# FNet mixing and a SoLU block on one core: three moves in the order of the steps

## The chip, the cores and the metric

The kernel runs on one core of a Trainium2 chip. The metric is the device time of one execution in microseconds. All times below are microseconds unless they say ns. The engines are named as in the profile: PE (TensorE, matmuls) with PEld (its weight loads), DVE (VectorE), ACT (ScalarE), POOL (GpSimd), and SP (SyncE, which here only issues DMAs).

## The reference

The first part is a Fourier mixing of `x`, 8 batches of 3136 rows by 256 features; its real part, as 25088 rows, goes through a block with 1024 hidden features.

```
X = fft(fft(x, axis=1), axis=2).real            # (8, 3136, 256) -> 25088 rows
h = X @ w_in                                    # 256 -> 1024
solu = h * softmax(h)
ln = (solu - mean) / sqrt(var + 1e-6) * g_ln
out = ln @ w_out                                # 1024 -> 256
```

All is in fp32.

## The kernel before, in words

**Pairs and units.** Two batches are a pair; there are four, numbered 0 to 3 in the code (`pairs`, and in the text here). The transform over the 3136 rows is split as 49 x 64. The *first transform* (length 49) is a matmul of the folded input with the table `F`; the *second* (length 64, with twiddles, table `T`) gives for one frequency `k1` the 128 x 256 tile `q`. Symmetry leaves 25 values of `k1`, so a pair has 25 *units* and the kernel 100. A unit stands for two results (`signs` 0 and 1), save for `k1 = 0`, which has one.

**Steps.** The program is one list of steps, written out by hand (`tc.manual_schedule()`): each engine runs its instructions in the order in which the code names them. Step `i` treats unit `i` in its middle part and other units in other parts. Steps 0 to 4 (`whole` is 4) form a first loop in which finished tiles are transposed on PE; from step 5 on the second loop runs:

- PE: `up` (two matmul groups, `h = q W_in`, line 272, into two PSUM banks); the second transform of unit `i + 2` (line 244); the product with `w_out` of unit `i - 5` (`Down`, line 446), as seven smaller products p1 to p7 by Strassen's scheme, in the order p1, p4, p5, (first transform), p6, p2, p3, p7.
- DVE: `even` (`ev`, line 278), two `join`s (line 286), two operations that finish an output (lines 503 and 505), the fold of a part of a chunk (below), two products (line 301), and a transpose in blocks (line 372).
- ACT: exponentials (294), squares (308), copies out of PSUM.
- POOL: the mirror of a part of a chunk, the four sums `S` of unit `i - 4` that p5, p6, p3 and p7 of the next step read (line 439), `rs`, and DMAs with indices.
- SP: in every even step `move_blocks` issues 16 DMAs (uT<-v, 128 KB each, line 408), in every odd one the output stores; also the DMAs named below. All of SP's DMAs go in the order in which they are issued.

`up` of the next step needs both PSUM banks free: the first after `ev`, the second after the second join.

**The next pair's first transform.** It runs inside the steps of the pair before. The rows of a pair are cut into 8 chunks (`NC`); chunk `c` has a start step `SUMS[p][c]`, two steps after the chunk before it. With `a` the step minus this start:

- `a` 0 and 1: POOL adds the mirrored rows, half a chunk in each (`add_mirror`, line 142). Each waits for the last product of the unit before (`behind`).
- `a` 1 and 2: DVE folds the features of that half (`fold_part`: lines 149, 150 and 174), and ACT copies one column.
- `a` 2: the load of chunk `c + 2` is issued, `xa` on SP (line 125) and `xb` on POOL (line 127). Chunks 0 and 1 are loaded at the first step of the pair before.
- `a` 3 and 4: PE transforms the halves (`transform1`, line 216), into one PSUM bank that the second transform uses too; ACT copies the result to `z`, and after the second half SP stores the chunk to a buffer in DRAM (`keep`, zd<-z, line 224).

`ahead` is called with "mirror", "fold" and "load". In steps 0 to 3 all three are called at the end of the step; in step 4 the mirror is called ahead of the block transpose (`turn_both`), and fold and load at the end.

**Turn.** `turn` reads the buffer in DRAM back with other axes on the partitions (g<-zd, line 232, issued on POOL), five values of `k1` at a time. The first is issued at the end of the step that lies 4 ahead of the pair's first (steps 21, 46 and 71); the second transform reads it two steps later (23, 48 and 73).

With start steps 3, 27 and 53, the halves of chunk 7 are transformed in steps 20 and 21 for pair 1, in 44 and 45 for pair 2, and in 70 and 71 for pair 3.

Of the kernel before, what the change touches and what calls it, by code (L numbers as in the profile page):

```python
# [26 lines left out]
NC = NH // CH  # L27
# [16 lines left out]
def kernel(  # L44
# [139 lines left out]
    def transform1(pr, s):  # L184

        c, l = divmod(2 * s, CH)
        if s == 0:
            pr.zd = dram.tile([ZR, NH, D], FP32, tag="zd", name="zd")  # L190
        if l == 0:

            if pr.p or c < 2:
                pr.z = zpool.tile([ZR, CH, D], FP32, tag="z", name="z")
            elif c < 4:
                if c == 2:
                    pr.z_u = fpool.tile([P, 2, FF], FP32, tag="u", name="z_u", bufs=1)
                pr.z = pr.z_u[0:ZR, c - 2].rearrange("p (l d) -> p l d", l=CH)
            elif c < 6:
                pr.z = Ws.rearrange("p (h w) c k -> h p (w c k)", h=2)[c - 4, 0:ZR].rearrange("p (l d) -> p l d", l=CH)  # L200
            elif c == 6:
                pr.z = S_tiles[1][0:ZR, 0:2].rearrange("p a c k -> p (a c k)").rearrange("p (l d) -> p l d", l=CH)
            else:
                pr.z = gpool.tile([P, KG, D], FP32, tag="g", name="z_g")[0:ZR, 0:CH, :]
            pr.zs[c] = pr.z
        y = pr.y[c]
        ps = result(0 if pr.p else s).rearrange("p (l d) -> p l d", l=2)
        if s == NH // 2 - 1:
            parts = [(ps[0:ZR, 0], y[:, l], 0), (ps[0:ZR, 1], pr.y0[:, 0], 1), (ps[0:ZR, 1], y[:, l + 1], 2)]
        else:  # L210
            parts = [(ps[0:ZR], y[:, l : l + 2], 0)]
        pr.done.append(s)
        first = True
        for o, i, t in parts:
            for h, cs in enumerate((EVEN, ODD)):
                nc.tensor.matmul(o[..., cs], F[:, 2 * t + h, :], i[..., cs], start=first, stop=True,  # L216
                                 skip_group_check=True)
                first = False
        nc.scalar.copy(pr.z[:, l : l + 2, :], ps[0:ZR])
        if l == CH - 2:  # L220
            keep(pr, c, slice(0, ZR if pr.p else 4 * KG))
# [295 lines left out]
    def first_out(t):  # L517
        if t.w == 0:
            t.batch.out = fpool.tile([P, 2, D], FP32, tag="ot0", name="ot0", bufs=2)
        return t.batch.out[:, t.w]  # L520

    def scale(t, s, ps):
        t.ot[s] = fpool.tile([P, D], FP32, tag="ot1", name="ot1", bufs=3) if s else first_out(t)
        nc.scalar.mul(out=t.ot[s], in_=ps, mul=t.rs[:, s : s + 1])
# [170 lines left out]

    SUMS = [None] + [[f + 2 * c for c in range(NC)] for f in (3, 27, 53)]

    def ahead(pr, i, work, after=None):  # L700

        for c in range(NC):
            a = i - SUMS[pr.p][c]
            if work == "load" and (i == (pr.p - 1) * NK and c < 2 or a == 2 and c + 2 < NC):
# [9 lines left out]
                          mybir.DependencyInfo(mybir.DependencyClass.Sync, mybir.DependencyReason.DATA),  # L714
                          reason="two operands at a time from SBUF")

    def ahead_pe(pr, i):

        for c in range(NC):
            half = i - SUMS[pr.p][c] - 3  # L720
            if half in (0, 1):
                transform1(pr, c * CH // 2 + half)

# [6 lines left out]
    with tc.manual_schedule():  # L730
# [80 lines left out]
        whole = WHOLE  # L811
# [21 lines left out]
        def other_pairs(i, do, *a):  # L833
            cur = units[i]
            if cur.p + 1 < NP:
                do(pairs[cur.p + 1], i, *a)
# [3 lines left out]
        for i in range(whole + 1):  # L840
            cur = units[i]
            prv = units[i - 1] if i else None
            if prv:
                turn_whole(prv)
            for s in cur.signs:
                join(cur, s)
            if prv and i < whole:
                for o, ps in prv.wait:
                    nc.vector.tensor_copy(out=o, in_=ps)
            for s in cur.signs:  # L850
                expo(cur, s)
            if prv and i == whole:
                for o, ps in prv.wait:
                    nc.scalar.copy(o, ps)
            if i == 0:

                weights.narrow_out(3)
            for s in cur.signs:
                product(cur, s)
                if i < whole and s == 0:  # L860
                    square(cur, s)
            if i == 1:
                weights.centre()
                weight_sums()
            if i < whole:

                begin(i + 1)
                if 1 in cur.signs:
                    square(cur, 1)
                stats(cur)  # L870
                power(cur)
            else:
                for s in cur.signs:
                    square(cur, s)
                other_pairs(i, ahead, "mirror", cur)
                turn_both(cur)
                stats(cur)
                power(cur)
            if i == 0:
                turn(first, 1, nc.sync)  # L880
            for work in ("mirror", "fold", "load") if i < whole else ("fold", "load"):
                other_pairs(i, ahead, work)

        def by_seven(i):
# [6 lines left out]
        for i in range(whole + 1, len(units) + lag + 1):  # L891
            cur = units[i] if i < len(units) else None
            prv = units[i - 1] if whole < i - 1 < len(units) else None
            old = units[i - lag] if i < len(units) + lag else None
            seven = by_seven(i - lag)
            kept = units[i - lag - 1] if i >= lag + 1 else None

            if kept:
                store(kept, 0)
            if cur:  # L900
                enter(i)
                even(cur, up(cur, 0))
                cur.odd = up(cur, 1)
                second_transform(i + 2)
            if seven:
                new = Down(old, fresh)
                fresh = False
                new.p1()
                new.seed()
            if i == len(units):  # L910
                for s in prv.signs:
                    square(prv, s)
            if prv:
                stats(prv)
            if seven:
                new.p4()
                new.p5()
                new.keep_p()
            elif old:
                plain = [(s, down(old, s, result(s + 1)[:, 0:D])) for s in old.signs]  # L920
            if cur:
                other_pairs(i, ahead_pe)
            if seven:
                new.p6()
                new.keep_x()
                new.p2()
                new.keep_c()
            elif old:
                for s, ps in plain:
                    scale(old, s, ps)  # L930
            if prv and prv.batch.shared and prv.w:
                prv.batch.mix()
            if cur:
                for s in cur.signs:
                    join(cur, s)
            if seven:
                new.p3()
                new.p7()
                new.finish()
            if cur:  # L940
                other_pairs(i, ahead, "mirror")
            if by_seven(i + 1 - lag):
                sums(units[i + 1 - lag], prv, nc.vector if i > len(units) else nc.gpsimd)
            if i % 2 == 0 and whole < i - 1 < len(units) - 2:
                batches[i // 2 - 1].place()
                move_blocks(batches[i // 2 - 1], slice(0, 2))
            if prv:
                power(prv)
            if kept and 1 in kept.signs:
                store(kept, 1)  # L950
            if cur:
                other_pairs(i, ahead, "fold")
                for s in cur.signs:
                    expo(cur, s)
                for s in cur.signs:
                    product(cur, s)
                if i < len(units) - 1:
                    for s in cur.signs:
                        square(cur, s)
                turn_both(cur)  # L960
                if cur.p == 0 and i in (5, 8, 11):
                    turn(first, (i + 1) // 3)
                for pr in pairs[1:]:
                    turn_parts(pr, i - pr.p * NK)
                other_pairs(i, ahead, "load")
            if i in (len(units), len(units) + 1):
                w = i - len(units)
                if w == 0:
                    batches[-1].place()
                move_blocks(batches[-1], slice(w, w + 1), (nc.sync, nc.gpsimd) if w else (nc.sync,))  # L970
# [82 lines left out]
```

## Time and profile before

| | |
|---|---|
| median of 3 runs | 1151.1 (1149.79 to 1153.33) |
| the profiled execution | 1150.92 |
| its span, first to last instruction | 1149.1 |
| mean granted clock of PE | 0.994 |
| a step with a first transform / without | 11.0 / 10.13 |
| busy share PE / DVE / ACT / POOL | 96% / 86% / 70% / 70% |

A row of the timeline gives the start in us, the duration in us, the engine, the line, the operation, output<-input, the shapes and a count; in brackets stands the engine's idle time ahead of it and what ended that. A row of the waits gives the engine, the line and tile, what it waited for, then the total in us, how often, and the longest. A row of the chain gives start, duration and what the end of the program hung on at that time. The step lengths are the distances between the first `up` matmuls of neighbouring steps.

### The profile page before, as it was taken

The numbers are of one execution on the slowest core, as the hardware profiler recorded it, in microseconds if no ns is written. First come the engines' busy times: TensorE is split into PE (matmuls) and PEld (weight loads), VectorE is DVE, ScalarE is ACT, GpSimd is POOL, SyncE is SP. The second block draws the span as 40 slices with busy tenths as digits, with TensorE's granted clock in tenths as the row PEclk, the third lists the DMA queues.
The fourth block names the chain that finished last, engine by engine and source line by source line (L and its number), as shares of the span: only waits on it lengthen the run. The fifth ranks groups of instructions, "written<-read, shape, count | busy, mean of one in ns | idle before, by whom it ended". The sixth has DMA issues, their size and how long they took to land.

```text
span 1149.1 us, 21936 instructions
## 1 busy us (share of the span) xinstructions
PE 1098.1 (96%) x7026; PEld 877.3 (76%) x7026; DVE 993.0 (86%) x1440; ACT 799.3 (70%) x1945; POOL 799.9 (70%) x698
## 2 busy tenths in 40 slices
PE   2988999999899999999999999999989999999998
PEld 1555787887688778778888787877868778888887
DVE  7889898898789988988888998898878999898983
ACT  4567777777566777777766777777766777777761
POOL 3036788875786888876778788876498576766673
PEclk9999999999999999999999999999999999999999
DMA  9772698776878779966869798876587676865664
GB/s 237 208 193 56 147 193 199 179 150 145 157 162 170 196 171 182 192 152 147 168 142 196 162 193 186 198 178 149 128 149 152 141 158 133 148 142 113 141 138 116
DMA packets 459889, 185.78 MB, mean 162 GB/s; under 512 B 427158, under 2 KB 441758, under 8 KB 459776
## 3 DMA queue, kind: packets, MB, share of 16 engines
q1 hardware_dynamic: 446016, 146.23, 62.1%
q0 software_dynamic: 13760, 38.16, 12.6%
q8 instruction: 57, 0.93, 0.3%
q14 instruction: 56, 0.46, 0.1%
HBM read 44.78 MB, written 38.80 MB: 73 GB/s over the span
## 4 chain that ended last, share of the span: by engine, by line
PE 85%; DMA 5%; DVE 4%; issue 2%; ACT 2%; POOL 1%; SPq 1%; POOLq 0%; DVEq 0%
PE ps_m L446 49%; PE ps_h L272 27%; PE ps_m L216 4%; PE ps_m L244 4%; DMA room<-in_x_dram 2%; DMA g<-zd 1%; DVE h L286 1%; DVE u L301 1%; DMA F<-in_f_tab_dram 1%; ACT h L308 1%; PE wps L660 1%; POOL S L439 0%; DVE ev L278 0%; DVE y L150 0%; DMA zd<-z 0%
## 5 line engine op out<-in xcount | busy, mean ns | idle before, releaser
L272 PE MATMUL ps_h<-Wi,q 128*128 128x512 f32 x800 | 363.3, 596 | 7.7 <-DVE nmax L286 4.5
L439 POOL TENSOR_TENSOR S<-uT 128x512 f32<-128x512 f32 x186 | 240.0, 1290 | 97.4 <-DVE u L301 38.8
L446 PE MATMUL ps_m<-Ws,S 128*128 128x128 f32 x2304 | 297.0, 275 | 0.6 <-POOL xa L142 0.6
L446 PEld LDWEIGHTS ps_m<-Ws,S 128*128 128x128 f32 x2304 | 280.6, 192 | 3.9 <-POOL xa L142 0.7
L308 ACT ACTIVATE h<-u,usum 128x1024 f32<-128x1024 f32 x196 | 225.0, 1149 | 83.6 <-DVE u L301 81.3
L272 PEld LDWEIGHTS ps_h<-Wi,q 128*128 128x128 f32 x800 | 144.7, 191 | 155.4 <-issue 141.5
L301 DVE SCALAR_TENSOR_TENSOR u<-h,u 128x1024 f32<-128x1024 f32 x196 | 239.1, 1256 | 7.2 <-ACT u L294 7.1
L294 ACT ACTIVATE u<-h,nmax 128x1024 f32<-128x1024 f32 x196 | 223.3, 1141 | 8.8 <-DVE nmax L286 5.8
L372 DVE STREAM_TRANSPOSE v<-u 128x2048 f32<-128x2048 f32 x88 | 203.4, 2311 | 3.0
L446 PE MATMUL ps_m<-Wo,uT 128*128 128x128 f32 x1536 | 205.0, 277 | 0.4 <-DMA out_dram<-ot 0.4
L446 PEld LDWEIGHTS ps_m<-Wo,uT 128*128 128x128 f32 x1536 | 188.9, 193 | 1.5 <-issue 1.5
L286 DVE CUSTOM_DVE_ANT_0 h<-ev,ps_h 128x1024 f32<-128x1024 f32 x100 | 122.1, 1221 | 17.3 <-DVE ev L278 8.6
L531 POOL DMA_INDIRECT out_dram<-ot,idx x96 | 109.5, 1141 | 36.5 <-issue 11.3
L286 DVE CUSTOM_DVE_ANT_0 h<-h,ps_h 128x1024 f32<-128x1024 f32 x96 | 117.3, 1221 | 13.8
L278 DVE SCALAR_TENSOR_TENSOR ev<-w_mid,r,ps_h 128x1024 f32<-128x1024 f32 x100 | 124.1, 1241 | 2.9 <-ACT S L589 2.4
L439 POOL TENSOR_TENSOR S<-S,uT 128x512 f32<-128x512 f32 x93 | 120.6, 1297 | 7.3
L439 POOL TENSOR_TENSOR S<-uT,S 128x512 f32<-128x512 f32 x93 | 119.7, 1287 | 7.3
L244 PEld LDWEIGHTS ps_m<-T,g 128*128 128x128 f32 x400 | 60.0, 191 | 60.1 <-issue 55.9
L446 PE MATMUL ps_m<-Ws,uT 128*128 128x128 f32 x768 | 103.6, 279 | 0.0
L446 PE MATMUL ps_m<-Wo,S 128*128 128x128 f32 x768 | 101.5, 275 | 0.8 <-ACT ot L481 0.8
L216 PE MATMUL ps_m<-y,F 98*100 98x258 f32 (+3 forms) x288 | 72.8, 389 | 23.9 <-DVE y L162 23.9
L446 PEld LDWEIGHTS ps_m<-Ws,uT 128*128 128x128 f32 x768 | 95.6, 195 | 0.0
(101 smaller groups left out, 1174.3 us busy)
## 6 DMA issues: line engine op xcount, KB each, us to landing
uT<-v SPq DMA_DIRECT2D x752, 128.0 KB
g<-zd POOLq DMA_DIRECT2D x72, 160.0 KB, 4.6
out_dram<-ot SPq DMA_DIRECT2D x176, 64.0 KB
xa<-in_x_dram SPq DMA_DIRECT2D x28, 392.0 KB
zd<-z SPq DMA_DIRECT2D x24, 400.0 KB
raw_in<-in_moe_w_in_dram SPq DMA_DIRECT2D x4, 512.0 KB
raw_out<-in_moe_w_out_dram SPq DMA_DIRECT2D x2, 1024.0 KB
r<-q SPq DMA_DIRECT2D x100, 0.5 KB
```

The costliest lines, as they stand in the source:

```text
L216: nc.tensor.matmul(o[..., cs], F[:, 2 * t + h, :], i[..., cs], start=first, stop=True, skip_group_check=True)
L244: nc.tensor.matmul(o, g[:, k, h * P : (h + 1) * P], table, start=(h == 0), stop=True, skip_group_check=True)
L272: nc.tensor.matmul(ps[:, fs], t.q[:, c * P : (c + 1) * P], Wi[:, c, fs], start=True, stop=True)
L278: nc.vector.scalar_tensor_tensor(out=t.ev, in0=w_mid, scalar=t.r, in1=ps, op0=ALU.mult, op1=ALU.add)
L286: nc.vector.tensor_tensor_reduce(out=t.h[s], in0=t.h[0] if s else t.ev, in1=t.odd, scale=1.0 if s else -0.5, scalar=3.0e38, op0=ALU.add, o ...
L294: nc.scalar.activation(out=t.u[s], in_=t.h[s], func=ACT.Exp, bias=t.nmax[:, s : s + 1], scale=-1.0, accum_out=t.esum[:, s : s + 1])
L301: t.last = nc.vector.scalar_tensor_tensor(out=t.u[s], in0=t.h[s], scalar=-1.0, in1=t.u[s], op0=ALU.mult, op1=ALU.mult, accum_out=t.usum[:, ...
L308: nc.scalar.activation(out=t.h[s], in_=t.u[s], func=ACT.Square, bias=t.usum[:, s : s + 1], scale=-float(FF), accum_out=t.ssq[:, s : s + 1])
L372: nc.vector.transpose(out=t.batch.v[:, :, t.w], in_=t.both.rearrange("p s (g n) -> p (s g) n", n=32))
L439: i = engine.tensor_tensor(out=S[j], in0=a, in1=b, op=op)
L446: nc.tensor.matmul(o, a[:, c], b[:, c], start=start and c == 0, stop=c == n - 1, skip_group_check=True)
L531: dma = nc.gpsimd.indirect_dma_start(out=out, out_offset=bass.IndirectOffsetOnAxis(ap=idx[:, i : i + 1], axis=0), in_=t.ot[s], in_offset=None)
```

## The change

- The last chunk's two halves of the first transform are issued in one step: the first half where it was, the second ("late") behind p2 of the same step, for all three pairs. The store of that chunk follows one step sooner than before.
- In step 4 the fold of half a chunk of pair 1 is issued ahead of the products of `u`, not at the end of the step.
- Pair 3's chunks start one step sooner: its start steps are 52, 54 and so on up to 66 in place of 53 up to 67.

Chunk 7 of pair 1 is then transformed in step 20, of pair 2 in 44, and of pair 3 in 69.

```
-    SUMS = [None] + [[f + 2 * c for c in range(NC)] for f in (3, 27, 53)]
+    SUMS = [None] + [[f + 2 * c for c in range(NC)] for f in (3, 27, 52)]
...
-    def ahead_pe(pr, i):
+    def ahead_pe(pr, i, late=False):
         for c in range(NC):
             half = i - SUMS[pr.p][c] - 3
+            if c == NC - 1:
+                half = int(late) if half == 0 else None
+            elif late:
+                half = None
             if half in (0, 1):
                 transform1(pr, c * CH // 2 + half)
...
+            if i == whole:
+                other_pairs(i, ahead, "fold")
             for s in cur.signs:
                 product(cur, s)
...
-            for work in ("mirror", "fold", "load") if i < whole else ("fold", "load"):
+            for work in ("mirror", "fold", "load") if i < whole else ("load",):
                 other_pairs(i, ahead, work)
...
             elif old:
                 for s, ps in plain:
                     scale(old, s, ps)
+            if cur:
+                other_pairs(i, ahead_pe, True)
             if prv and prv.batch.shared and prv.w:
                 prv.batch.mix()
```

More of the change, by code (lines that the diff above doesn't have):

```diff
@@ L692, in centre @@
             nc.vector.tensor_tensor(out=Wo, in0=Wo, in1=wbar.unsqueeze(1).to_broadcast([P, KF, D]), op=ALU.subtract)
-    SUMS = [None] + [[f + 2 * c for c in range(NC)] for f in (3, 27, 53)]
+    SUMS = [None] + [[f + 2 * c for c in range(NC)] for f in (3, 27, 52)]
     def ahead(pr, i, work, after=None):
@@ L715, in behind, with ahead_pe @@
                           reason="two operands at a time from SBUF")
-    def ahead_pe(pr, i):
+    def ahead_pe(pr, i, late=False):
         for c in range(NC):
             half = i - SUMS[pr.p][c] - 3
+            if c == NC - 1:
+                half = int(late) if half == 0 else None
+            elif late:
+                half = None
             if half in (0, 1):
@@ L857 @@
                 weights.narrow_out(3)
+            if i == whole:
+                other_pairs(i, ahead, "fold")
             for s in cur.signs:
@@ L880 @@
                 turn(first, 1, nc.sync)
-            for work in ("mirror", "fold", "load") if i < whole else ("fold", "load"):
+            for work in ("mirror", "fold", "load") if i < whole else ("load",):
                 other_pairs(i, ahead, work)
@@ L930 @@
                     scale(old, s, ps)
+            if cur:
+                other_pairs(i, ahead_pe, True)
             if prv and prv.batch.shared and prv.w:
```

## The prediction

> **What bounds the kernel now.** I read the page first, its busy rows and its chain.
>
> ```profile
> PE 1098.1 (96%) x7026; PEld 877.3 (76%) x7026; DVE 993.0 (86%) x1440; ACT 799.3 (70%) x1945; POOL 799.9 (70%) x698
> PE 85%; DMA 5%; DVE 4%; issue 2%; ACT 2%; POOL 1%; SPq 1%; POOLq 0%; DVEq 0%
> ```
>
> PE sets the time, so only a stretch in which PE waits can be won. Behind the start, PE's waits are two:
>
> ```profile
> PE ps_m L244 <- DMA g<-zd: 8.9, 2, 4.8
> ...
> PE ps_h L272 <- DVE ev L278: 2.9, 1, 2.9
> ```
>
> The g<-zd waits stand in steps 23 and 73, where the second transform reads the first `g` of pairs 1 and 3. The timeline of PE around the first:
>
> ```profile
> 294.11 3.60 PE L272 MATMUL ps_h<-Wi,q 128*128 128x512 f32 x8
> 302.51 0.68 PE L244 MATMUL ps_m<-T,g 128*128 128x128 f32 x4 [4.81 <-DMA g<-zd]
> 303.03 1.86 PE L446 MATMUL ps_m<-Wo,uT 128*128 128x128 f32 x8
> ...
> 310.91 3.60 PE L272 MATMUL ps_h<-Wi,q 128*128 128x512 f32 x8
> ```
>
> and the chain:
>
> ```profile
> 288.41 4.35 DMA zd<-z
> ...
> 294.88 7.39 DMA g<-zd
> ```
>
> Chunk 7's second half (12 matmuls at 279.08) is copied to `z` by 281.2, but its store goes out at 288.41, since SP was issuing 16 uT moves and 4 output stores from 270.97 to 287.7. `turn` waits on POOL until 293.05, and `g` lands at 302.3. PE lost more than the 4.81: eight matmuls then took 1.86 where they otherwise take 1.06, at half the granted clock.
>
> The 2.9 is at the start of step 6. The DVE timeline ahead of it, with the same three fold operations one step later:
>
> ```profile
> 100.46 0.60 DVE L149 TENSOR_TENSOR y<-xa 98x254 f32<-98x254 f32 x1
> 100.98 1.72 DVE L150 TENSOR_TENSOR y<-xa 98x254 f32<-98x254 f32 x1
> 102.63 1.23 DVE L174 TENSOR_TENSOR y<-xa,xb 98x2 f32<-98x2 f32 x1
> 103.78 1.27 DVE L278 SCALAR_TENSOR_TENSOR ev<-w_mid,r,ps_h 128x1024 f32<-128x1024 f32 x1
> ...
> 107.74 0.42 DVE L149 TENSOR_TENSOR y<-xa 98x254 f32<-98x254 f32 x1
> 108.08 0.41 DVE L150 TENSOR_TENSOR y<-xa 98x254 f32<-98x254 f32 x1
> 108.41 0.15 DVE L174 TENSOR_TENSOR y<-xa,xb 98x2 f32<-98x2 f32 x1
> ```
>
> 3.32 us against 0.74. The slow ones ran while POOL did two-operand work (mirror to 100.78, then `S`). PE stood from 102.15 to 105.11 for `ev`.
>
> **Part 1: both halves of chunk 7 in one step.** For pair 1 they move from steps 20 and 21 into 20. The store is then issued in step 20 ahead of that step's moves (270.97), lands by about 278, and `turn` at step 21's end (POOL free at 282.5) waits for nothing; with 2.4 to issue and 7.4 for the transfer `g` is there at 292.3, and PE wants it at 297.6. Step 23 lasted 310.91 - 294.11 = 16.80; its neighbours last 10.13. Gain 6.67. For pair 3, step 73 lasted 849.80 - 833.74 = 16.06: gain 5.93. Pair 2, whose last half already has a spare step, shows no wait (its step lasts 10.13), so nothing is late next.
>
> What it adds: the second half's 1.32 us of PE leaves step 21 for step 20, no work more. It waits for ACT's copy of the first half out of the same bank, done at 269.74; p6 and p2 (1.79 us) hide that, as PE comes to it at 270.7; without that cover it costs up to 1 us in each of three steps. I take 0, bounds 0 to 3. On SP the 16 moves of steps 20 and 44 now queue behind this store, some 2.4 us of issue and 3.5 of packets; `S` is formed from them about 5 us later, at 292, and p5 of step 23 reads it at 299.8: hidden, with 7 us to spare.
>
> **Part 2: step 4's fold ahead of the products.** Its input, the mirror at 94.36, ends at 95.63, so the fold runs from 95.7 to 96.45, uncontended (0.74), and the first product starts 0.64 later than its 95.81. `ev` starts at 103.78 - 3.32 + 0.64 = 101.10, 2.68 sooner. Its ACT copy (0.18) falls behind two copies and ahead of squares that wait for the products anyway. PE's wait shrinks to 0.3, and the eight matmuls at 105.11 no longer take 5.38 at half clock: up to 3.5. Against it, POOL's mirror, which waits for the products, starts 0.64 later while DVE is 2.7 sooner, so POOL's sums meet the next fold and products: down to 2.0. I take 3.0.
>
> **Part 3: pair 3 one step sooner.** This changes the parity. Its loads move from odd steps to even ones, and in an even step SP issues the 16 moves first. Queues passed: SP (`xa`, and the `zd` stores, which now precede the moves), POOL (`xb`, mirrors). How late a load behind the moves lands shows in the loads of step 50, on SP:
>
> ```profile
> 596.47 15.64 SPq L408 DMA_DIRECT2D uT<-v  x16
> 612.15 1.70 SPq L125 DMA_DIRECT2D xa<-in_x_dram  x2
> ```
>
> and two mirrors, on POOL:
>
> ```profile
> 694.97 1.28 POOL L142 TENSOR_TENSOR xa<-xa,xb 98x510 f32<-98x510 f32 x1 [0.36 <-DVE u L301]
> ...
> 706.34 1.27 POOL L142 TENSOR_TENSOR xa<-xa,xb 98x510 f32<-98x510 f32 x1 [1.87 <-DMA xa<-in_x_dram]
> ```
>
> Today the load of step 59 goes out at 697.95 and its mirror in step 61 already waits 1.87 for it: 8.4 to land (with a `zd` store just ahead of it); the load at 656.81 was there within 5.2; the pair at 612.15 took about 9. After the change the load of step 58 follows that step's moves, at 694.3, and with 6.5 (bounds 5 and 9) lands at 700.8, but the mirror of step 60 wants to start at 694.97. POOL stands 5.8 us, and behind the mirror queue the four sums (5.2 us), `rs`, an output store and `xb`. PE doesn't want these sums before 708.0; they would end at 707.2, so PE is not held directly. DVE is: the sums move from 696.2-701.4 to 702.0-707.2, onto DVE's fold and products at 702.8-705.9. What such a meeting costs stands in step 22, where POOL was late for another reason:
>
> ```profile
> 295.09 2.75 DVE L301 SCALAR_TENSOR_TENSOR u<-h,u 128x1024 f32<-128x1024 f32 x1 [0.30 <-ACT u L294]
> ...
> 297.77 2.28 DVE L301 SCALAR_TENSOR_TENSOR u<-h,u 128x1024 f32<-128x1024 f32 x1
> ```
>
> Undisturbed each is 1.22, so 2.6 for two products, and 2.6 for three folds (above). With two or three sums overlapping, 2 to 4 us per even step; I take 3. DVE wins back what it now waits for PE, 0.39 + 0.47 a step, 1.7 in two, and it has a reserve: its second join of step 61 ends at 712.16 and PE wants that bank at 714.9, so 2.7. Seven mirrors are hit (steps 52 and 56 to 66; step 54's load is early): 7 x (3 - 1.7) - 2.7 = 6.4; bounds 7 x 0.3 - 2.7, so 0, and 7 x 2.3 - 2.7 = 13.4. I take 6.5; a longer step brings the load earlier in it, which holds against the upper end. One first half falls into step 55, where PE idles 0.88: a gain of 0 to 0.9, taken as 0 since DVE is late there.
>
> [...]
>
> **Sum.** -6.67 - 5.93 - 3.0 + 6.5 = -9.1. The profiled execution took 1150.92 (span 1149.1); the median is 1151.1, 0.2 more. 1151.1 - 9.1 = 1142.0.
>
> **Rivals.** *The load costs nothing*: it lands within 5, or DVE's reserve takes up the meetings. For it, the load of 656.81; against it, the wait at 706.34 with a sooner issue. -15.6: 1135.5.
>
> *The meetings eat the gain*: four us an even step, term 11 to 16, with part 2 at 2.0 (-14.6 in all without the term). For it, the fold's 3.32; against it, that longer steps relieve it. With 13.4 it is 1150.
>
> *Slower*: the late `ev` makes PE wait long enough for its clock to halve. A wait of 2.95 did that (3.41 us at 0.5, a loss of 1.7), one of 0.88 at 648.7 did not. If meetings of 4 us give PE waits of over about 2 us in five or more steps between 54 and 67, the term is 13.4 + 5 x 1.7 = 22: slower by 6, 1157. It decides where DVE loses over 4 us in two steps.
>
> [...]
>
> *The stalls stay*: `turn` is issued where it was, so a store that is still late would keep 12.6; pair 2 speaks against it. It is within the second rival.
>
> **How the numbers follow.** Forecast (term 3 to 10) 0.42; load costs nothing 0.25; gain eaten 0.19; slower 0.14. What a measurement can tell is 0.3%, 3.45 us. The first two are faster by more (0.67), the third is within (0.19). The range runs from -15.6 with the 0.9 and part 2's other 0.5 added (1134) to the upper end of the third case (1152.5); the slower case is left out. The forecast's own range is 1138.5 to 1145.5.
>
> **What would show it.** Right: no L244 wait on g<-zd, steps 23 and 73 at 10.13; the wait on `ev` at the start of step 6 gone; in pair 3 the mirrors of even steps waiting 4 to 8 us for `xa`, products of 2.3 and more between steps 53 and 67, and those steps over 11.0. Wrong: these products still 1.22, which leaves the first rival; half clock between 630 and 760, the slower one.

## The result and the profile after

The kernel after took 1154.75 in the median of 7 runs (1151.4 to 1158.47), the kernel before, run beside it, 1150.58 (1145.97 to 1153.33). The ratio is 1.0033, with a 95% interval of 1.0017 to 1.0050: a little slower, where 1142.0 was forecast. The profiled execution took 1155.61, its span is 1153.6 (before: 1149.1).

The distances between the first `up` matmuls, summed over stretches, show where the 4.5 between the two spans arose:

| stretch | before | after | difference |
|---|---|---|---|
| start to step 6 | 105.1 | 102.9 | -2.2 |
| steps 22 to 24 | 37.1 | 30.4 | -6.7 |
| steps 25 to 43 | 203.9 | 204.7 | +0.8 |
| steps 50 to 72 | 245.9 | 264.7 | +18.8 |
| steps 73 to 75 | 36.3 | 30.4 | -5.9 |
| all else | 520.8 | 520.5 | -0.3 |

The gains came nearly as forecast; the price of moving pair 3 was almost three times the forecast 6.5. The page after, its busy row and its chain:

```profile
PE 1101.2 (95%) x7026; PEld 879.6 (76%) x7026; DVE 1011.3 (88%) x1440; ACT 797.1 (69%) x1945; POOL 801.8 (69%) x698
...
PE 77%; DMA 6%; SPq 6%; DVE 4%; issue 3%; POOL 2%; ACT 1%; POOLq 0%; DVEq 0%; ACTq 0%
```

PE carried 85% of the chain before and carries 77% now; SP's queue (1% before) and POOL have come in. The two waits for `g<-zd` are gone from the list of PE's waits, and two others stand there (total, times, longest):

```profile
PE ps_m L216 <- ACT q L250: 6.4, 5, 2.5
PE ps_m L446 <- issue: 6.1, 2, 4.6
...
PE ps_h L272 <- DVE ev L278: 1.3, 2, 1.1
...
PE ps_m L446 <- POOL S L439: 0.8, 2, 0.6
```

**Step 23 and step 5.** The timeline of PE in step 23: the second transform follows `up` without a wait, and the next `up` comes 10.13 after the first (302.07 - 291.94; before 16.80).

```profile
291.94 3.60 PE L272 MATMUL ps_h<-Wi,q 128*128 128x512 f32 x8
295.37 0.61 PE L244 MATMUL ps_m<-T,g 128*128 128x128 f32 x4
...
302.07 3.60 PE L272 MATMUL ps_h<-Wi,q 128*128 128x512 f32 x8
```

The timeline of DVE in the last step of the first loop: the three fold operations take 0.84 together (96.21 to 97.05) ahead of the product, where they took 3.32 behind the transpose, and `ev` starts at 101.60 (before 103.78); counted from the first `up` of step 5, that is 8.4 in place of 11.1.

```profile
96.21 0.42 DVE L149 TENSOR_TENSOR y<-xa 98x254 f32<-98x254 f32 x1 [0.30 <-POOL xa L142]
96.55 0.42 DVE L150 TENSOR_TENSOR y<-xa 98x254 f32<-98x254 f32 x1
96.89 0.16 DVE L174 TENSOR_TENSOR y<-xa,xb 98x2 f32<-98x2 f32 x1
96.96 1.22 DVE L301 SCALAR_TENSOR_TENSOR u<-h,u 128x1024 f32<-128x1024 f32 x1
...
101.60 1.24 DVE L278 SCALAR_TENSOR_TENSOR ev<-w_mid,r,ps_h 128x1024 f32<-128x1024 f32 x1
```

**Pair 3's chunks.** SP's queue, with the load of chunk 2 (issued for step 54, used by the mirror of step 56): it goes out behind the sixteen moves.

```profile
636.93 14.27 SPq L408 DMA_DIRECT2D uT<-v  x16
651.31 0.92 SPq L125 DMA_DIRECT2D xa<-in_x_dram  x1
```

POOL's mirrors of pair 3, in brackets POOL's idle time ahead of each:

```profile
614.18 1.27 POOL L142 TENSOR_TENSOR xa<-xa,xb 98x510 f32<-98x510 f32 x1 [10.02 <-DMA out_dram<-ot]
622.61 1.28 POOL L142 TENSOR_TENSOR xa<-xa,xb 98x510 f32<-98x510 f32 x1
...
657.16 1.26 POOL L142 TENSOR_TENSOR xa<-xa,xb 98x510 f32<-98x510 f32 x1 [6.77 <-DMA out_dram<-ot]
670.56 1.28 POOL L142 TENSOR_TENSOR xa<-xa,xb 98x510 f32<-98x510 f32 x1
682.21 1.26 POOL L142 TENSOR_TENSOR xa<-xa,xb 98x510 f32<-98x510 f32 x1 [2.91 <-DMA xa<-in_x_dram]
```

The first mirror of a chunk waits, the second doesn't. POOL was free for the one at 657.16 from 650.39, before its load had even been issued (651.31). The list names a store of the output there, which ended at about the same time, but the load's 98 packets of 4 KB run from 653 to 657 in the trace, so the mirror starts when they are in; at 682.21 the list names the load itself. Three more mirrors waited 3.65 (703.86), 5.05 (729.45) and 5.93 (775.54). What DVE then does while PE is in step 54, with a mirror and the sums `S` pushed onto its fold and products:

```profile
622.36 3.04 DVE L149 TENSOR_TENSOR y<-xa 98x254 f32<-98x254 f32 x1
625.32 1.48 DVE L150 TENSOR_TENSOR y<-xa 98x254 f32<-98x254 f32 x1
626.73 1.22 DVE L174 TENSOR_TENSOR y<-xa,xb 98x2 f32<-98x2 f32 x1
627.87 1.21 DVE L301 SCALAR_TENSOR_TENSOR u<-h,u 128x1024 f32<-128x1024 f32 x1
...
629.01 2.27 DVE L301 SCALAR_TENSOR_TENSOR u<-h,u 128x1024 f32<-128x1024 f32 x1
```

The fold took 5.59 (622.36 to 627.95) in place of about 0.8. So far this is as forecast. The next rows are not; ACT at the same time:

```profile
629.12 1.15 ACT L308 ACTIVATE h<-u,usum 128x1024 f32<-128x1024 f32 x1 [6.23 <-DVE u L301]
...
631.33 1.15 ACT L308 ACTIVATE h<-u,usum 128x1024 f32<-128x1024 f32 x1 [0.97 <-DVE u L301]
...
632.48 0.35 ACT L250 COPY q<-ps_m 128x256 f32<-128x256 f32 x1
632.73 0.27 ACT L472 COPY ps_m<-ps_m 128x128 f32<-128x128 f32 x1
```

and PE, in step 54 and in step 57:

```profile
627.42 1.06 PE L446 MATMUL ps_m<-Ws,S 128*128 128x128 f32 x8
633.09 1.20 PE L446 MATMUL ps_m<-Ws,S 128*128 128x128 f32 x4 [4.61 <-issue]
...
667.45 1.24 PE L216 MATMUL ps_m<-y,F 98*100 98x258 f32 x4 [2.16 <-ACT q L250]
```

ACT idles 6.23 until the first late product is done, then squares. Behind the squares, in ACT's order, stand the copy of `q` out of PSUM (line 250) and the copy that seeds a later product of `Down` (line 472). The seed ends at 633.0, PE resumes at 633.09 after 4.61. In step 57 it is the copy of `q`, from a bank that the first transform reuses: done at 667.39, PE resumes at 667.45. PE's clock then ran at half for 6.8 from 630.7, 3.4 from 668.3 and 3.4 from 740.0, and nowhere else between 37 and the last microsecond.

Step lengths, with those of before in brackets: step 53 11.5 (10.1), 54 17.1 (10.1), 57 15.0 (11.0), 63 15.3 (11.0). These four make 16.7 of the 18.8; no other of steps 50 to 72 differs by more than 1.4.

### The profile page after: what moved, and what is told of

It reads as the page before. It is cut to its first block, busy times and chain, and to the rows that moved or that the text cites. A ratio compares the mean times of both kernels' runs of the same rounds, so it can differ in the third digit from the quotient of the medians.

```text
span 1153.6 us, 21932 instructions
## 1 busy us (share of the span) xinstructions
PE 1101.2 (95%) x7026; PEld 879.6 (76%) x7026; DVE 1011.3 (88%) x1440; ACT 797.1 (69%) x1945; POOL 801.8 (69%) x698
## 4 chain that ended last, share of the span: by engine, by line
PE 77%; DMA 6%; SPq 6%; DVE 4%; issue 3%; POOL 2%; ACT 1%; POOLq 0%; DVEq 0%; ACTq 0%
PE ps_m L446 46%; PE ps_h L272 23%; SPq L408 4%; PE ps_m L216 4%; PE ps_m L244 3%; DMA room<-in_x_dram 2%; DVE u L301 2%; DMA uT<-v 1%; POOL S L439 1%; DMA out_dram<-ot 1%; ACT h L308 1%; DVE h L286 1%; DMA F<-in_f_tab_dram 1%; SPq L224 1%; DMA xa<-in_x_dram 1%
## 5 line engine op out<-in xcount | busy, mean ns | idle before, releaser
L439 POOL TENSOR_TENSOR S<-uT 128x512 f32<-128x512 f32 x186 | 242.5, 1304 | 108.2 <-DVE u L301 34.4
L446 PEld LDWEIGHTS ps_m<-Ws,S 128*128 128x128 f32 x2304 | 282.3, 193 | 10.9 <-issue 6.4
L142 POOL TENSOR_TENSOR xa<-xa,xb 98x510 f32<-98x510 f32 (+1 forms) x48 | 59.5, 1241 | 62.4 <-DMA out_dram<-ot 32.9
```

The source lines that it names most:

```text
L439: i = engine.tensor_tensor(out=S[j], in0=a, in1=b, op=op)
L446: nc.tensor.matmul(o, a[:, c], b[:, c], start=start and c == 0, stop=c == n - 1, skip_group_check=True)
```

## The experiments

The theory was, from the rows above: moving pair 3 by *one* step puts its loads into even steps, behind the moves; the mirrors are late, their sums delay DVE, and that reaches PE through ACT's queue and then through the clock. The rivals: the price lies in one of the other two parts; or in pair 3 being sooner at all, onto the last steps of pair 2; or in the place of pair 3 in the program rather than in the parity.

**Each part alone.** Four kernels beside one another; the kernel before took 1150.26 in the median of 17 runs beside them. `e1_without_shift`, from the kernel after:

```
-    SUMS = ... for f in (3, 27, 52)]
+    SUMS = ... for f in (3, 27, 53)]
```

> The changed kernel with pair 3's start steps back at 53. Theory: the shift by one step costs all of the loss (steps 52 to 72 lengthen by 18.9 in the changed kernel's profile), so without it only gains stay: 6.7 in step 23, 5.9 in step 73 and about 2 around step 5, some 14 to 15 below before, near 1136, with steps 53 to 69 at 10.1 and 11.0. Rival: the two halves in one step upset SP's queue in pair 3 (the store ahead of the moves), and the steps from 54 on stay long: then it stays within 4 of before.

Measured: 1136.73 (1134.6 to 1142.65), ratio 0.9892 [0.9864, 0.9919]. Steps 53 to 69 have the lengths of before (245.9 for steps 50 to 72), and the mean granted clock of the profiled execution is 1.000 (0.994 in the kernels before and after). Three of its mirrors of pair 3, with POOL's idle time:

```profile
644.08 1.28 POOL L142 TENSOR_TENSOR xa<-xa,xb 98x510 f32<-98x510 f32 x1 [0.36 <-DVE u L301]
...
654.18 1.27 POOL L142 TENSOR_TENSOR xa<-xa,xb 98x510 f32<-98x510 f32 x1 [0.25 <-DVE u L301]
...
699.59 1.27 POOL L142 TENSOR_TENSOR xa<-xa,xb 98x510 f32<-98x510 f32 x1 [2.92 <-DMA xa<-in_x_dram]
```

The first two don't wait for data. The third and two others (678.14 and 721.17) wait 0.9 to 2.9 for their load, but they start 4.8 to 5.8 after the start of their step and no step is longer for it. Without the shift the change is worth about 13.

`e2_shift_alone` is the kernel before with the one line of the shift (53 becomes 52).

> The kernel before with pair 3's start steps at 52 and nothing else. Theory: it pays the 18.9 in steps 52 to 72 and wins the 5.9 of step 73, because the last store comes a step sooner by itself; step 23 keeps its 16.8. Some 12 to 13 above before, near 1163. Rival (the shift is harmless by itself): 6 below before, 1145.

Measured: 1162.2, ratio 1.0100 [1.0078, 1.0122]. Steps 54 and 57 last 17.2 and 15.2; steps 50 to 72 take 262.7 in place of 245.9. Step 23 took 13.2 and not 16.8 as expected: PE waited 2.9 for `g` there, and the step is longer than its neighbours' 10.13 by little more than that wait (3.1). The shift alone also brings step 73 to 10.1, since pair 3's data is then a step sooner while its `turn` stays: that gain is in both parts, and the shift adds nothing to part 1 there.

`e3_one_step_alone` has only part 1, the two halves in one step.

> Only the two halves of chunk 7 in one step. Theory: steps 23 and 73 fall to 10.1, 12 to 12.6 below before, near 1138. Rival: the second half waits for the copy of the first and takes up to 1 us in three steps, or the sums behind the later moves come late: 8 or less below before.

Measured: 1141.18, ratio 0.9923 [0.9902, 0.9943]. Steps 23 and 73 last 10.1; step 5 is unchanged at 12.4.

`e4_fold_alone` has only part 2, the fold ahead of the products in step 4.

> Only step 4's fold ahead of the products. The prediction: 2.0 to 3.5 below before (3.0), so 1147.6. The changed kernel's profile gives 2.2 by the start of step 6 and loses 0 to 1 behind it: 1 to 2.5 below before. Rival: the saved wait is only shifted, no difference.

Measured: 1150.18, ratio 0.9990 [0.9970, 1.0010], not distinguishable from before. Step 5 does fall from 12.5 to 9.7, as in every profile with this part, but in this profile some is given back at `g`. PE's wait is no shorter than before (8.5 in all against 8.9),

```profile
PE ps_m L244 <- DMA g<-zd: 8.5, 2, 4.9
```

and steps 23 and 73 take 17.9 and 16.5 (before 16.8 and 16.1). Less the waits and twice the neighbours' 10.13, that leaves 5.6 lost in the two (before 3.7, with PE at half clock for 3.4 at each). With both other waits gone the fold may be worth more: e1, which has it, took 4.5 less than e3, which hasn't, though their intervals overlap. So by the times its worth lies somewhere from 0 to about 4.5. The profiles say more of its own place: steps 5 and 6 together take 22.9 with it (the kernel after, e1 and e4), 25.0 without it in e2 and e3, and 25.6 before.

**The loads and the queue.** Four kernels, each made from the kernel after; the kernel before took 1151.08 in the median of 17 runs beside them. `e5_first_loads_sooner` loads pair 3's first two chunks at step 49 in place of step 50:

```
-            if work == "load" and (i == (pr.p - 1) * NK and c < 2 or ...):
+            if work == "load" and (i == (pr.p - 1) * NK and c < 2 and pr.p < 3 or ...):
...
+                if i == 2 * NK - 1:
+                    for c in range(2):
+                        load(pairs[3], c)
```

> The changed kernel with the loads of pair 3's first two chunks issued in step 49, ahead of step 50's moves; the other loads stay in even steps behind the moves. Theory (a load behind the moves makes the mirror late): mirror 52 starts on time, steps 53 and 54 fall from 11.5 and 17.1 to 10.1, step 55 by up to 0.9; steps 57 to 59 and 63 stay long. 8 to 9 below the changed kernel, near 1146. Rival (POOL has too much to do in these steps whatever the load): steps 53 and 54 stay.

Measured: 1146.07, ratio 0.9953 [0.9935, 0.9970]. Steps 53 and 54 are back at 10.1, while steps 57 (14.7) and 63 (17.8), whose loads still follow the moves, stay long. The price goes from the steps whose loads now come in time and stays in those whose loads are late. The profiled execution was the slowest of the seven (1153.41): step 63 took 2.4 more than in the kernel after, and step 29, which the edit doesn't touch, 14.5 (11.1 before), with a wait of 2.4; its mean granted clock was 0.994, that of the other six 0.997 or 0.998.

`e6_loads_on_act_queue` issues pair 3's `xa` loads on ACT's DMA queue.

```
-        nc.sync.dma_start(out=xa, ...)
+        (nc.scalar if pr.p == 3 else nc.sync).dma_start(out=xa, ...)
```

> The changed kernel with all of pair 3's xa loads issued on ACT's DMA queue instead of SP's, in the same steps. Theory (queueing behind the moves on SP is the cause): every mirror of an even step finds its data, steps 53 to 69 fall to 10.1 and 11.0, and the time to that of the kernel without the shift, near 1137. Rival (the DMA engines themselves are full with the moves, whichever queue): the loads land as late, the mirrors wait 3 us and more, and the time stays over 1148.

Measured: 1209.51, ratio 1.0515 [1.0495, 1.0536]: far from both. The first mirror (611.39) now finds its data there, but the moves are late. SP's queue, where 16 moves took 14.27 in the kernel after, and POOL's largest wait:

```profile
566.26 31.95 SPq L408 DMA_DIRECT2D uT<-v  x16
```

```profile
POOL S L439 <- DMA uT<-v: 71.7, 16, 10.1
```

One late transfer is exchanged for another, so the run tells nothing of the cause. Why SP's issues took 31.95 stays open; the two loads on ACT's queue went out at 589.46, within that stretch. The rows of the other runs say something of the rival that the DMA engines are full: from issue to mirror the loads behind the moves took 5.1 to 9.2 in the kernel after, and those of odd steps whose mirrors waited for them 7.7 to 8.4 (before and e1). So they are not slower under way; they go out too late. Counted from the start of the even step, the loads of chunks 2 to 7 go out 3 to 9 sooner than before, but their mirrors are due a whole step, 11, sooner.

`e7_squares_behind_seed` puts the squares behind the copies of `q` and of the seed on ACT, by calling them in the next step:

```
-            if i == len(units):
+            if prv:
...
-                if i < len(units) - 1:
-                    for s in cur.signs:
-                        square(cur, s)
```

> The changed kernel with a unit's squares on ACT moved to the next step, behind the copy of q and the seed copy, so that these two no longer queue behind squares that wait for late products. Theory (PE's waits come through ACT's queue): the waits of PE on q (6.4 in 5) and on the seed (4.6 in step 54) go, with the half clock they cause; about 8 to 12 below the changed kernel, 1143 to 1147, though the mirrors stay late and the products long. Rival (PE is held by ev and the joins, the path that the prediction priced): as slow as the changed kernel, with PE waiting on DVE instead.

Measured: 1165.28, ratio 1.0118 [1.0095, 1.0140]: a miss. The wait of the first transform for `q` has gone from the list, and steps 57 and 63 fall to 11.0 and 11.4. But an output copy (line 481) now stands behind the squares, and PE waits for that instead, in 45 steps:

```profile
PE ps_m L446 <- ACT ot L481: 17.8, 45, 3.5
```

Steps without a first transform rise from 10.1 to 10.6 all through the program, and steps 59 and 60 to 13.7 and 12.4. Steps 50 to 72 take 262.8, hardly less than the 264.7 of the kernel after. So the order on ACT decides *where* the lateness strikes PE; taking one path away doesn't take the lateness away.

`e8_pair2_even` leaves pair 3 at 53 and moves pair 2 instead, from 27 to 28, so that its loads fall into even steps.

> The changed kernel with pair 3 back at 53 and pair 2 at 28 in place of 27: pair 2's loads of chunks 2 to 7 now fall in even steps (its first two stay in step 25). Theory (parity against the moves): pair 2 loses what pair 3 loses in steps 56 to 69 of the changed kernel, about 10, near 1147. Rival (the loss is pair 3's place, one step nearer to the pair before): near 1137, as without the shift.

Measured: 1146.23, ratio 0.9965 [0.9950, 0.9980], by the two ratios some 8 more than e1. Steps 25 to 43 take 212.4 (203.9 before), and PE waits 7.1 in eight places for the copy of `q`. The price follows the parity to another pair.

**Two steps sooner.** `e9_two_steps_sooner` is e5 with pair 3 at 51 and the first loads in step 48: odd again, as before the change, and sooner than after it. The kernel before took 1148.79 in 9 runs beside it.

```
-    SUMS = ... for f in (3, 27, 52)]
+    SUMS = ... for f in (3, 27, 51)]
...
-                if i == 2 * NK - 1:
+                if i == 2 * NK - 2:
```

> The kernel after, with the fourth pair's column sums from step 51 (52 in the kernel after, 53 before) and the loads of its first two chunks in step 48, so that its chunks are again loaded in odd steps, mirrored in even ones and summed in odd ones as in the kernel before, but two steps sooner. Theory (what costs is the parity: in the kernel after the loads of later chunks are issued in even steps, behind the rows of uT, and land late): steps 53 to 69 stay at 10.1 to 11.0, the wait of TensorE for ScalarE's copy of q does not show, and the time is about that of the kernel with the sums at step 53, 1135 to 1139. Rival (being sooner than before is what costs, since the fourth pair's sums then meet the third pair's last steps and second transform): 1148 or more, with long steps near 51 to 57.

Measured: 1137.66 (1136.25 to 1139.98), ratio 0.9911 [0.9891, 0.9930]. Being sooner costs next to nothing (steps 50 to 72 take 247.6; before 245.9); being in even steps does. SP's queue, where the loads go out ahead of the next moves:

```profile
626.27 0.51 SPq L125 DMA_DIRECT2D xa<-in_x_dram  x1
...
630.52 13.31 SPq L408 DMA_DIRECT2D uT<-v  x16
...
648.97 0.34 SPq L125 DMA_DIRECT2D xa<-in_x_dram  x1
```

The mirrors that use these two chunks (636.01 and 656.57) wait 0 and 1.17 for data, where those of the same chunks in the kernel after waited 6.77 and 2.91. POOL idles 3.58 and 2.39 ahead of two later ones (679.73 and 700.52), which costs no step anything: they start 5.9 and 4.7 after the start of their step. Step 53 takes 12.5 (10.1 in e1), by the one wait of PE that is left there. This version and e1 beat both kernels; their intervals overlap, so neither is shown to be the better.

## Why the prediction was wrong

**Part 1 was right**: -6.67 and -5.93 were forecast, -6.7 and -5.9 came; the second halves' wait and the store ahead of the moves cost nothing that shows (steps 20 and 21 take 22.4 together in both kernels).

**Part 2 was right in its place**: step 5 is 2.8 shorter and step 6 as long as before, 3.0 was forecast. As a time of its own it could not be shown.

**Part 3 was mis-sized: 6.5 with an upper bound of 13.4, against 18.8.** The mechanism in it held up to DVE: even steps' loads come late (5.1 to 9.2 from issue to mirror; 6.5 was taken), six of the seven mirrors wait 2.9 to 10.0 (that of step 64 doesn't), products take 2.27. Step 54 came out wrong, though: its own mirror did wait for nothing, as forecast, but POOL was still late from the mirror of step 52. The step of the working that failed is the price of DVE's lateness for PE: 3 a meeting, less 1.7 that DVE wins back over two steps, and once the reserve of 2.7 at the second join. ("PE is not held directly", said of the sums, nearly held: PE waited 0.8 for them.) That reserve is the one on the way from DVE to PE through `up`, and along it PE didn't wait at all in steps 50 to 72. The shorter way runs through ACT. In the timelines of before, step 60 has ACT's copy of `q`

```profile
696.07 0.35 ACT L250 COPY q<-ps_m 128x256 f32<-128x256 f32 x1
```

and PE's first transform, which needs the bank that it empties:

```profile
697.74 1.03 PE L216 MATMUL ps_m<-y,F 98*100 98x258 f32 x4
```

The copy ends at 696.42, so the reserve is 1.3, and ACT had no slack ahead of it: the squares began the moment the products allowed it and ran straight into the copy. Counted from the first `up` of the step, the second product of steps 57, 58, 59, 63 and 67 ends 3.6, 2.2, 2.1, 3.9 and 2.1 later in the kernel after than before, and PE's first transform waits 2.16, 0.80, 0.67, 2.45 and 0.66: each time the lateness less 1.4, in the same step, with nothing won back first. In steps 60, 61 and 64, where the product is 0.7 to 1.3 late, PE doesn't wait. The lateness itself was sized about right (3 was taken; behind the mirrors of steps 56 to 66 at most 3.9 came), save for the first meeting, which made the product 6.6 late in step 54. The first half in step 55 gained nothing, as taken: steps 55 and 56 last 19.7 together (19.6 before), and the 0.88 stood in step 56.

**The clock was named, but in a rival; the forecast's sum had nothing for it.** "Slower" had PE waits halve the clock and gave 1157 at 0.14; its place (`ev`) was wrong, its size close. In the three stretches at half clock, 13.6 in all, PE was busy 11.3; half of that, 5.6 of the 18.8, is what the clock cost by this estimate, and about 13 are waits. PE's rows in steps 50 to 72 give it somewhat more: 7.5 of added busy time (252.5, before 245.0) and 11.4 of added idle time (12.3, before 0.9). The rival asked for five steps with waits of over 2; waits in three were enough, since the longest were larger.

**The relief by longer steps was real**: behind the long steps 57 and 63 the next load went out 0.6 and 3.3 ahead of its mirror's step, and these mirrors waited 2.91 and not at all for it. What a mirror costs goes by its place in its step more than by its wait. In the profiles of the kernel after, e2 and e5 the mirrors of steps 56 to 66, due 3.8 after the start of the step, cost the next step nothing when they start up to 6.7 after it, 0.3 to 1.3 from 6.9 to 8.6, and 3.7 to 6.8 from 9.9 to 10.9.

## What to carry to other kernels

When periodic work is moved by one step, write down for each transfer what is ahead of it in its queue in the new step; here a shift by one step cost 18.8 and one by two steps 1.7. Reckon the reserve for each in-order engine on the way to the bottleneck, and take the smallest: a late vector result reached PE through copies queued behind its consumer on ACT, not through the engine's own next product (PE stood 4.61 for it in step 54). Add what a wait costs in clock, before calling a loss bounded: by the estimate above it was 5.6 of the 18.8 here.

## What the runs showed of the hardware

What a wait of PE cost in clock did not follow from the wait's length. In the clock records of the kernels before and after, six stretches are at half clock, the last of each program aside: 3.413 each from 105.1, 303.1 and 842.4 before, 6.827 from 630.7 and 3.413 each from 668.3 and 740.0 after. In the 3.413 ahead of each, by PE's matmul rows, whose ends are modelled, PE was busy 0.46, 0.57 and 0.99 before, 1.15, 1.25 and 0.96 after. The wait that each began in or followed was 2.95, 4.81 and 4.06 before, 4.61, 2.16 and 2.45 after.

Waits of about the same length went without such a loss. In e9, in whose step 53 PE waited about as long as in step 57 of the kernel after, the timeline of PE has

```profile
617.34 1.13 PE L446 MATMUL ps_m<-Ws,S 128*128 128x128 f32 x8 [2.10 <-issue]
```

The eight matmuls behind these 2.10 took 1.13 and the next eight 1.06; behind the 2.16 of the kernel after, eight took 1.92 at half clock (at 668.48). In e3 the wait of 2.95 ahead of step 6 was followed by four matmuls in 1.98, as were the 0.20 in the kernel after; before, the clock stood at half for 3.413 behind the same 2.95. Around `g` too the loss differed: step 23 took 16.8 before and 17.9 in e4, and no wait for `g` in e4 was longer than 4.9. So what a wait would cost in clock could not be told from its length here.
